# Weight loads on SP, a DMA pipe in the planner, and another order of layer 2's attention sessions

## The chip, the cores and the metric

The kernel runs on one core of one Trainium2 chip. The metric is the device time of one execution in microseconds (us), lower is better. Names of engines: PE multiplies matrices (TensorE), ACT computes exponentials and other functions (ScalarE), DVE works on vectors (VectorE), POOL is GpSimd, SP issues transfers (SyncE).

## The reference, cut to what matters

```python
def reference(A_x, A_wqkv, A_wo, B_x, B_w1, B_w2, B_w3, B_w4):
    # A(x): 16 heads of 28, softmax(q k^T / sqrt(28)) v, then @ wo        x: 1 x 2048 x 448
    # B(x): h = gelu(layernorm(x) @ w1); the four quarters of h's columns are shifted
    #       by -1, +1, -2, +2 rows; x1 = x + shifted @ w2
    #       x1 + gelu(layernorm(x1) @ w3) @ w4                            w3: 448 x 1792
    x = A_x
    x = x + A(layernorm(x))
    x = x + B(layernorm(x))
    x = x + A(layernorm(x))        # the same weights again
    x = x + B(layernorm(x))
    return x
```

So there are two layers, each an attention over 2048 rows and a mixing MLP. All data are bfloat16 in memory; `gelu` is the tanh form.

## The kernel before, in words

**Tiles.** The 2048 rows are 16 tiles of 128. Heads are padded from 28 to 32 rows, so four heads fill 128 partitions; the 16 heads are four groups g = 0 to 3. Queries are taken in chunks of up to 512 columns (`CHUNKS`: tiles 0-3, 4-7, 8-11, 12-13, 14-15), keys in chunks of their own (`KC`; in layer 2 tiles 0-2, 3-6, 7-10, 11-12, 13-15).

**Scores and exponentials.** A block is 128 keys (256 for the two half-width query chunks) of one head against one query chunk: 128 x 512 scores. The kernel has 2048 such blocks. PE writes the scores to PSUM (L1353) and an exponential turns them into bfloat16 weights (L1591). The blocks go in *units*: an even unit takes three PSUM banks (0-2), an odd unit two (3-4), and one ACT instruction handles a unit. A unit's scores wait until the exponential of the unit before last has read its banks, so PE is at most two units ahead. PE then multiplies the weights with the values (L802, `t_pv`).

**Blocks on DVE.** A few blocks get their exponential from DVE, in five instructions (`d_first`, `d_chain`: L1435, L1462, L1464, L1466, L1469). `D_RATE` says how many per query chunk; they use banks 6 and 7. `R_RATE` gives further ones, which borrow bank 2 of an even unit, so that this unit has two blocks for ACT and one for DVE.

**Sessions.** `ORDER` lists for each layer triples (query chunk, first key tile, end of key tiles). Each triple gives four sessions, one per head group; the kernel has 68, numbered from 0, and layer 2 begins at session 32. A session over part of the keys leaves partial sums: they are spilled to memory (`uscr<-ub`) and reloaded (`ub<-uscr`) when the next session of the same queries runs. The softmax uses an upper bound of the scores instead of their maximum. It is made from the largest key norms of all key chunks that the session touches or has touched (`t_bias`, L1295 to L1302). When a later session of the same queries needs the bound over more chunks, the queries are shifted by the difference first (`t_db`, `t_qp`, L1326, L1328, L1375). A key chunk therefore goes through projection on PE, eviction by DVE (L1152), squares on POOL (L1138), sums on PE and a maximum on DVE (L1165) before the first session with its bound can start.

**From layer 1 to layer 2.** When a tile leaves layer 1's MLP (`t_w4`: products with w4, residual sum L2035), its mean and variance are taken (L990, L991, and L996, L998 on POOL), it is normalized (L1005), transposed by a DMA issued by SP (L1015, or L1123 through memory) and projected to keys and values of layer 2 (`k_proj`, `v_proj`).

**MLP.** `t_mixA` and `t_mixB` make h and the w3 product. While attention runs, the GELU of a whole tile group is one long ACT instruction (L2019), with loads of function tables around it; h goes through tanh (L1839), whose table holds the exponential too. After the last exponential (the tail) the GELU works directly on PSUM (L1994).

**What sets the order.** Nothing is ordered by hand. When the kernel is built, a planner (`Sched.run`) runs all these routines as coroutines against a list of durations and readiness times, picks the next instruction for each engine by readiness and rank (`RANK`, `Q_LEAD`), and so fixes one instruction list per engine, with semaphore waits. On the chip each engine works through its list in order. Where the planner expects PE to idle, it inserts fillers (L2065), small matmuls whose result is unused. `LSEG` names the sessions whose start releases the clearing of the padded wo and the two groups of weight loads. Each transfer has an issue time and a time to landing in the planner, independent of other transfers.

Of the kernel before, what the change touches and what calls it, by code (L numbers as in the profile page):

```python
# [184 lines left out]
class Sched:  # L185
# [12 lines left out]
    def __init__(self, P):  # L198
# [17 lines left out]
        self.port = {"dve": (0.0, 0.0), "pool": (0.0, 0.0)}  # L216
        self.fill = None
# [167 lines left out]
    def run(self):  # L385
        P = self.P
        while True:
# [141 lines left out]
ORDER = {0: [(0, 0, 4), (1, 0, 4), (0, 4, 8), (0, 8, 16), (1, 4, 16), (2, 0, 16), (3, 0, 16), (4, 0, 16)], 1: [(0, 0, 7), (1, 0, 7), (0, 7, 11), (1, 7, 11), (0, 11, 16), (1, 11, 16), (2, 0, 16), (3, 0, 16), (4, 0, 16)]}  # L529
# [8 lines left out]
R_RATE = {(0, 0): 0, (0, 1): 0.03, (0, 2): 0.01, (0, 3): 0.02, (0, 4): 0, (1, 0): 0, (1, 1): 0, (1, 2): 0, (1, 3): 0.01, (1, 4): 0}  # L538
RLO = 5
RHI = 7  # L540
RPRIO = 0.5
# [4 lines left out]
DHI = 8  # L546
DPK = 2
RANK = {('q', 0, 1): 1.1, ('b', 0, 1): 1.254, ('b', 0, 0): 2.155, ('a', 0, 0): 1.411, ('k', 1, 0): 1.354, ('q', 0, 3): 1.199, ('k', 0, 1): 1.4, ('k', 1, 2): 1.381, ('k', 0, 2): 1.351, ('b', 0, 3): 2.679, ('q', 0, 2): 2.465, ('a', 0, 1): 1.751, ('k', 1, 1): 1.553, ('q', 1, 0): 1.781, ('k', 0, 3): 1.671, ('q', 1, 1): 2.16, ('a', 0, 2): 1.954, ('k', 1, 4): 1.95, ('a', 0, 4): 1.128, ('a', 0, 3): 1.842, ('b', 0, 4): 2.343, ('b', 0, 2): 2.033, ('a', 1, 0): 2.46, ('b', 1, 0): 1.514, ('a', 1, 3): 2.355, ('b', 1, 4): 1.667, ('a', 1, 2): 2.471, ('k', 1, 3): 2.435, ('a', 1, 1): 2.773, ('q', 1, 2): 2.611, ('b', 1, 2): 2.547, ('a', 1, 4): 2.738, ('b', 1, 3): 2.923, ('q', 1, 3): 2.432, ('b', 1, 1): 2.728, ('c', 0, 1): 1.22, ('w', 0, 1): 1.216, ('c', 0, 0): 1.023, ('w', 0, 0): 1.428, ('o', 0, 0): 1.775, ('v', 1, 0): 2.261, ('l', 1, 0): 2.465, ('v', 0, 1): 2.442, ('v', 1, 2): 1.73, ('l', 1, 2): 2.614, ('v', 0, 2): 1.5, ('c', 0, 3): 1.184, ('w', 0, 3): 1.412, ('o', 0, 1): 2.321, ('v', 1, 1): 1.973, ('l', 1, 1): 1.656, ('v', 0, 3): 2.178, ('o', 0, 2): 1.033, ('v', 1, 4): 2.482, ('l', 1, 4): 1.02, ('o', 0, 4): 1.711, ('o', 0, 3): 1.677, ('c', 0, 4): 2.197, ('w', 0, 4): 2.472, ('c', 0, 2): 2.133, ('w', 0, 2): 2.065, ('o', 1, 0): 1.617, ('c', 1, 0): 2.936, ('w', 1, 0): 1.115, ('o', 1, 3): 1.429, ('c', 1, 4): 2.839, ('w', 1, 4): 2.075, ('o', 1, 2): 2.017, ('v', 1, 3): 1.122, ('l', 1, 3): 2.584, ('o', 1, 1): 2.122, ('c', 1, 2): 2.188, ('w', 1, 2): 2.465, ('o', 1, 4): 2.837, ('c', 1, 3): 2.566, ('w', 1, 3): 2.092, ('c', 1, 1): 2.723, ('w', 1, 1): 2.8}
Q_LEAD = {(0, 1): 10, (0, 2): 5, (0, 3): 6, (1, 0): 4, (1, 1): 8, (1, 2): 5, (1, 3): 9}
D_RATE = {(0, 0): 0.11, (0, 1): 0.1, (0, 2): 0.07, (0, 3): 0, (0, 4): 0, (1, 0): 0.005, (1, 1): 0.105, (1, 2): 0.03, (1, 3): 0.02, (1, 4): 0}  # L550
PE_NORM = {(0, 0): False, (0, 1): False, (0, 2): False, (0, 3): False, (0, 4): False, (1, 0): False, (1, 1): False, (1, 2): False, (1, 3): True, (1, 4): True}
TANHW = {(0, 0): 0, (0, 3): 0, (0, 7): 0, (0, 11): 0, (0, 13): 0, (1, 0): 0, (1, 3): 0, (1, 7): 0, (1, 11): 0}
# [8 lines left out]
LSEG = (4, 7, 9)  # L561
POOLED = ('sq', 'otn', 'z2', 'xx')
GMERGE = {}
WARM = 0.5
# [9 lines left out]


def DRATE(L, ch, g):
    return D_RATE.get((L, ch), 0)

# [5 lines left out]
def build_kernel(nc, A_x, A_wqkv, A_wo, B_x, B_w1, B_w2, B_w3, B_w4, out, n_layers=2):  # L584
# [79 lines left out]
    with st:  # L664
# [103 lines left out]
        def op(eng, dur, fn, reads=(), writes=(), **kw):  # L768
            if eng == "pool" or (eng == "dve" and kw.pop("two", False)):
                kw["port"] = True  # L770
            return (eng, dur, fn, list(reads), list(writes), kw)
# [52 lines left out]
        def t_load():  # L824
# [24 lines left out]
            yield ("wait", ("segstart", LSEG[1]))  # L849
            for j in range(4):  # L850
                yield dma("pool", lambda e, j=j: e.dma_start(out=wo_pad[32 * j:32 * j + DH, :, :], in_=wo_v[j]), reads=[("woz",)], writes=[(("wo_pad",), j)], t=8.0, iss=0.7)
            yield dma("pool", lambda e: e.dma_start(out=w1[:, 0:3, :], in_=B_w1[0:384, :].rearrange("(c p) n -> p c n", p=128)), writes=[(("w1",), 0)], t=8.0, iss=0.7)
            yield dma("pool", lambda e: e.dma_start(out=w1[0:64, 3, :], in_=B_w1[384:448, :]), writes=[(("w1",), 1)], t=8.0, iss=0.7)
            yield dma("pool", lambda e: e.dma_start(out=w2[:, :, :], in_=B_w2.rearrange("(c p) n -> p c n", p=112)), writes=[("w2",)], t=8.0, iss=0.7)
# [158 lines left out]
        def tr_dma(slot, xt, i):  # L1013
            k = num(slot)
            return dma("sp", lambda e: e.dma_start_transpose(out=xv(xt)[:, :, 128 * i:128 * i + 128], in_=xn[:, k, :]),  # L1015
                       reads=[("xn", k)], writes=[(("xT", xt), i)], t=TR_T, iss=1.2, touch=[slot])
# [294 lines left out]
        def t_fct(L, p, pp):  # L1311
            i = PI[L, (pp, p)]
            for g in range(4):
                yield ("spawn", t_db(L, p, pp, g), 1)
# [850 lines left out]
```

## Time and profile before

| what | us |
|---|---|
| median of 3 runs (lowest, highest) | 1064.53 (1062.19, 1065.12) |
| the profiled execution | 1063.28 |
| its span in the profile | 1061.5 |
| ACT busy | 1007.3 (95%) |
| PE busy, fillers included | 990.9 (93%) |
| DVE busy | 680.6 (64%) |
| POOL busy | 306.0 (29%) |

Read busy times as averages: the kernel has a start, a long middle of attention with MLP work between, and a tail without exponentials. A row of a group gives line, engine, operation, output and inputs with shapes, count, then busy time, mean length of one in ns, and the idle time before these instructions with what ended it. The 40 digits of an engine are its busy tenths in 40 equal slices of the span.

### The profile page before, as it was taken

Reading aid. Unit: us, or ns where it says so; the run is one execution under the profiler, and the core shown is the slowest. Engines: PE = TensorE matmul, PEld = TensorE weight load, DVE = VectorE, ACT = ScalarE, POOL = GpSimd, SP = SyncE. Lnnn points to the kernel's source line nnn. Section 1 sums busy time; section 2 is a strip of 40 time slices with the busy share of each in tenths; the row PEclk is TensorE's granted clock in tenths of the full one; section 3 lists DMA queues with packets and bytes.
Section 4 is the critical chain, followed back from the end, with each engine's and each line's share of the span. In section 5 each row is a group of like instructions: output and inputs, shape, how many; then the busy total and the mean of one; then the engine's idle time right before and its main releaser. Section 6 shows DMA issues by size and latency. Waiting matters only on the chain.

```text
span 1061.5 us, 35381 instructions
## 1 busy us (share of the span) xinstructions
PE 990.9 (93%) x15980; PEld 410.0 (39%) x15983; DVE 680.6 (64%) x1365; ACT 1007.3 (95%) x913; POOL 306.0 (29%) x507
## 2 busy tenths in 40 slices
PE   8898998999999999999999989998989999899998
PEld 4332342333424334434432333343333343444465
DVE  7674797788568757776457445747778536565442
ACT  7998999999999999999999999999999999999952
POOL 2342112434232304453234111103554300432111
PEclk9999999999999999999999999999999999999999
DMA  4547232402121103231132114334412110121000
GB/s 117 130 117 202 76 72 68 62 22 37 21 75 41 33 12 86 63 52 23 33 78 74 44 52 129 104 76 116 74 23 32 32 39 25 34 66 25 12 21 24
DMA packets 96443, 64.22 MB, mean 61 GB/s; under 512 B 68580, under 2 KB 85172, under 8 KB 96292
## 3 DMA queue, kind: packets, MB, share of 16 engines
q1 hardware_dynamic: 92916, 53.88, 21.1%
q0 software_dynamic: 3376, 8.09, 2.8%
q8 instruction: 125, 2.05, 0.8%
q14 instruction: 26, 0.21, 0.1%
HBM read 28.03 MB, written 16.76 MB: 42 GB/s over the span
## 4 chain that ended last, share of the span: by engine, by line
ACT 72%; PE 20%; DMA 3%; DVE 3%; issue 1%; SPq 1%; POOL 0%; DVEq 0%
ACT PT L1591 66%; PE ps L811 11%; PE ps L1353 4%; PE ps L802 3%; ACT h2T L2019 2%; DMA xT<-xnd 2%; ACT fb L1839 1%; PE ps L2065 1%; ACT L2019 1%; DMA xT<-xn 1%; ACT L1591 1%; DVE fb L1462 0%; DMA rT<-ub 0%; DMA PT<-in_A_wqkv_dram 0%; SPq L1015 0%
## 5 line engine op out<-in xcount | busy, mean ns | idle before, releaser
L1591 ACT ACTIVATE PT<-ps 128x1024 bf16<-128x1024 f32 (+1 forms) x802 | 910.4, 1340 | 15.5 <-PE ps L1353 14.8
L1353 PE MATMUL ps<-qT,kT 32*128 32x512 bf16 (+1 forms) x2560 | 315.2, 341 | 36.8 <-ACT PT L1591 28.4
L802 PE MATMUL ps<-PT,vaug 128*32 128x512 bf16 (+1 forms) x2491 | 250.9, 342 | 0.8 <-ACT PT L1591 0.5
L1353 PEld LDWEIGHTS ps<-qT,kT 32*128 32x128 bf16 x2560 | 80.6, 91 | 317.6 <-ACT PT L1591 285.1
L811 PE MATMUL ps<-xT,w 128*32 128x512 bf16 (+4 forms) x2368 | 160.9, 345 | 5.8 <-DMA xT<-xn 4.0
L2065 PE MATMUL ps<-ident 128*32 128x256 bf16 x3212 | 145.9, 279 | 4.2 <-DVE hT L1820 2.4
L802 PEld LDWEIGHTS ps<-PT,vaug 128*32 128x32 bf16 x2491 | 74.2, 95 | 93.4 <-issue 76.8
L2065 PEld LDWEIGHTS ps<-ident 128*32 128x32 bf16 x3212 | 90.8, 98 | 31.9 <-issue 13.1
L811 PE MATMUL ps<-w,h2T 128*32 128x448 bf16 x1288 | 90.5, 358 | 5.7 <-ACT h2T L2019 5.7
L1696 POOL TENSOR_TENSOR otn<-ub,fb 128x512 bf16<-128x512 f32 (+1 forms) x35 | 39.9, 1139 | 187.7 <-DMA fb<-rscr 187.7
L1998 DVE CAST h2T<-ps 128x384 bf16<-128x384 f32 (+1 forms) x84 | 52.2, 622 | 50.8 <-PE ps L811 50.0
L811 PEld LDWEIGHTS ps<-xT,w 128*32 128x32 bf16 (+1 forms) x2368 | 64.6, 96 | 50.1 <-issue 27.2
L1138 POOL TENSOR_TENSOR sq<-kT 128x512 bf16<-128x512 bf16 (+2 forms) x32 | 31.2, 981 | 94.7 <-DVE kT L1152 80.4
L1837 POOL TENSOR_TENSOR fb<-hT 112x512 f32<-112x512 bf16 (+1 forms) x36 | 37.8, 1054 | 61.7 <-DVE hT L1820 53.7
L811 PEld LDWEIGHTS ps<-w,h2T 128*32 128x32 bf16 x1288 | 36.0, 97 | 34.9 <-issue 15.2
L811 PE MATMUL ps<-xT,wk_pad 128*32 128x512 bf16 (+2 forms) x576 | 44.6, 366 | 3.1 <-DMA xT<-xnd 3.0
L1923 POOL TENSOR_TENSOR x_res<-x_res,x1b 128x448 f32<-128x448 f32 x32 | 38.2, 1199 | 32.1 <-DVE xn L1010 32.1
L1435 DVE TENSOR_SCALAR yd<-ps 128x512 int32<-128x512 f32 x43 | 29.5, 687 | 25.6 <-PE ps L1353 25.2
L1138 POOL TENSOR_TENSOR sq<-qT 128x512 bf16<-128x512 bf16 x28 | 30.6, 1100 | 43.2 <-DVE qT L1187 36.2
L811 PE MATMUL ps<-wo_pad,otn 128*32 128x448 bf16 x512 | 39.5, 356 | 2.9 <-DVE x_res L1750 1.6
L811 PE MATMUL ps<-w,hT 112*32 112x448 bf16 x512 | 41.2, 355 | 0.5 <-DVE x1b L1908 0.5
L811 PE MATMUL ps<-xT,wq_pad 128*32 128x512 bf16 x448 | 39.3, 388 | 1.4 <-DMA xT<-xnd 0.9
(183 smaller groups left out, 1190.3 us busy)
## 6 DMA issues: line engine op xcount, KB each, us to landing
uscr<-ub SPq DMA_DIRECT2D x28, 256.0 KB, 2.0
ub<-uscr SPq DMA_DIRECT2D x28, 256.0 KB, 4.0
fb<-rscr SPq DMA_DIRECT2D x24, 256.0 KB
xnd<-xn SPq DMA_DIRECT2D x28, 128.0 KB, 2.1
x_res<-in_A_x_dram POOLq DMA_DIRECT2D x16, 224.0 KB, 2.7
xd<-x_res SPq DMA_DIRECT2D x16, 224.0 KB, 2.9
x_res<-xd SPq DMA_DIRECT2D x16, 224.0 KB, 3.6
out_dram<-obf SPq DMA_DIRECT2D x16, 112.0 KB, 1.7
```

Of the source, the lines that this page charges most:

```text
L802: return lambda e: e.matmul(out=out, lhsT=lhsT, rhs=rhs, start=start, stop=stop, **kw)
L811: r.append(e.matmul(out=out[c:c + w, :], lhsT=lhsT[:, c:c + w], rhs=rhs, start=start, stop=stop, tile_position=(0, c)))
L1138: return both("sq", 0.15 + NW * 0.0018, 0.07 + NW * 0.00104, lambda e: e.tensor_tensor(out=sq[:, si, 0:NW], in0=src, in1=src, op=ALU.mult) ...
L1353: yield op("pe", (0.005 + NW * 0.00042) / nc_, lambda e, i=i, kc=kc, j=j, g=g, a=a, NW=NW, bank=bank: e.matmul(out=ps[:, bank, i * NW:(i + ...
L1435: yield op("dve", c_ps(512), lambda e: e.tensor_scalar(out=y, in0=ps[:, bi(bank), :], scalar1=SCALE * L2E * FS, scalar2=-126.0 * FS, op0=A ...
L1591: yield op("act", 0.06 + n * w * 0.000833, lambda e, bk=bk, s0=s0, n=n, w=w: e.activation(out=PT[:, s0:s0 + n, 0:w], in_=ps[:, bk[0]:bk[0] ...
L1696: yield both("otn", 0.2 + NW * 0.0021, 0.07 + NW * 0.00104, lambda e: e.tensor_tensor(out=otn[:, g, 0:NW], in0=u, in1=rb[:, 0:NW], op=ALU. ...
L1837: yield both("z2", 0.2 + NW * 0.00165, 0.07 + NW * 0.00104, lambda e: e.tensor_tensor(out=f, in0=z, in1=z, op=ALU.mult), hk, [fk])
L1923: yield both("xx", 1.2, 0.54, lambda e: e.tensor_tensor(out=X, in0=X, in1=X1, op=ALU.add), [xk, ("x1b", s)], [xk], deps=[nop_])
L1998: ev = op("dve", c_ps(m * NW), lambda e, hr=hr, pv=pv: e.tensor_copy(out=hr, in_=pv), reads=[("ps", bi(b))], writes=hk, touch=[b])
L2019: yield op("act", c_act(len(fr_) * NW), lambda e, v=v: e.activation(out=v, in_=v, func=ACT.Gelu_apprx_tanh), reads=allk, writes=allk, tab= ...
L2065: return [e.matmul(out=ps[32 * c:32 * c + 32, bi(b), 0:256].rearrange("p (a n) -> p a n", n=128), lhsT=ident[:, 32 * c:32 * c + 32], rhs=i ...
```

## The change

- The four loads of wo, the three of w1 and w2, and the three of w3 and w4 are issued by SP instead of POOL; they start at sessions 6 and 10 instead of 7 and 9 (`LSEG`).
- The planner gets one DMA pipe: a transfer with a service time `svc` lands no earlier than the pipe has served it behind all others, and a transpose (`hold`) keeps its queue until the pipe is free.
- Layer 2's sessions (0,7,11), (1,7,11), (0,11,16) become (1,7,11), (0,7,16): 32 sessions in layer 2 instead of 36, 64 in all.
- In layer 2 the bounds and their differences are made for the four head groups together (`t_bias4`, `t_fct`) instead of one by one.
- `D_RATE` and `R_RATE` are given for each pair of sessions instead of each query chunk. Ranks, leads and some planner constants have other values; `DHI` lets a DVE block be chosen one step further ahead.
- `POOLED` keeps only the squares of keys and queries on POOL; three other operations may go to DVE where the planner finds that earlier.
- `TANHW[0, 11]`: the tile group 11, 12 of layer 1 takes the tanh form for its second GELU.
- `ONCE` is empty, so the branches that it opens are not used.

```diff
+        self.pipe = 0.0
...
             if dma:
-                self.cur[eng] = start + kw.get("iss", 0.35)
+                svc = kw.get("svc", 0.0)
+                self.cur[eng] = start + kw.get("iss", 0.4)
                 t_end = start + kw.get("dma_time", 3.0)
+                if svc:
+                    if kw.get("hold"):
+                        self.cur[eng] = max(self.cur[eng], self.pipe)
+                    self.pipe = max(self.pipe, start + 1.2) + svc
+                    t_end = max(t_end, self.pipe + 1.2)
...
-ORDER = {... 1: [(0, 0, 7), (1, 0, 7), (0, 7, 11), (1, 7, 11), (0, 11, 16), (1, 11, 16), (2, 0, 16), (3, 0, 16), (4, 0, 16)]}
+ORDER = {... 1: [(0, 0, 7), (1, 0, 7), (1, 7, 11), (0, 7, 16), (1, 11, 16), (2, 0, 16), (3, 0, 16), (4, 0, 16)]}
...
-DPRIO = 1.5
+DPRIO = 2
...
-R_RATE = {(0, 0): 0, (0, 1): 0.03, ...}
+R_RATE = {(0,): 0, (1,): 0.03, ..., (31,): 0}
...
-RPRIO = 0.5
+RPRIO = 1
...
-DHI = 8
+DHI = 9
...
-D_RATE = {(0, 0): 0.11, (0, 1): 0.1, ...}
+D_RATE = {(0,): 0.1, (1,): 0.125, ..., (31,): 0.12}
...
-TANHW = {... (0, 11): 0, ...}
+TANHW = {... (0, 11): 1, ...}
...
-LSEG = (4, 7, 9)
-POOLED = ('sq', 'otn', 'z2', 'xx')
+LSEG = (4, 6, 10)
+POOLED = ('sq',)
...
             yield ("wait", ("segstart", LSEG[1]))
+            yield ("wait", ("woz",))
             for j in range(4):
-                yield dma("pool", lambda e, j=j: e.dma_start(out=wo_pad[...], in_=wo_v[j]), ..., t=8.0, iss=0.7)
+                yield dma("sp", lambda e, j=j: e.dma_start(out=wo_pad[...], in_=wo_v[j]), ..., t=5.0, svc=0.35, iss=0.55)
...
             yield ("wait", ("segstart", LSEG[2]))
-            yield dma("pool", ... w3[:, 0:3, :] ..., t=16.0, iss=0.7)
+            yield dma("sp", ... w3[:, 0:3, :] ..., t=5.0, svc=4.9, iss=0.55)
...
+        def t_bias4(L, p):
+            yield ("wait", ("rtn",))
+            for g in range(4):
+                for c in range(p):
+                    yield ("wait", ("k", L, g, c))
...
+            if p > 1:
+                yield op("dve", 0.14, ... reduce_max(out=k2[:, L, p, :], in_=kmaxc[:, L, :, 0:p], axis=AX.X), ...)
...
+            yield op("dve", 0.13, ... tensor_tensor(out=sc[:, 5, :], in0=src, in1=RTN, op=ALU.mult), ...)
+            yield op("dve", 0.13, ... tensor_scalar(out=bcb[:, L, p, :], in0=sc[:, 5, :], scalar1=WSH, ...), ...)
+            yield op("dve", 0.13, ... tensor_scalar(out=bc29[:, L, p, :], in0=bcb[:, L, p, :], scalar1=M29, ...), ...)
+            for g in range(4):
+                yield ("sig", ("bc", L, p, g))
...
-                    rate = rates.get((L, ch), 0)
+                    rate = rates.get((si // 2,), 0)
```

More of the change, by code (lines that the diff above doesn't have):

```diff
@@ L560 @@
 SMALL = [11, 12]
[L561 to L562 removed]
+LSEG = (4, 6, 10)
+POOLED = ('sq',)
 GMERGE = {}
+ONCE = {}
 WARM = 0.5
@@ L1123, in load_xT @@
             yield dma("sp", lambda e: e.dma_start_transpose(out=xv(xt)[:, :, 0:128 * n], in_=xnd[128 * t0:128 * (t0 + n), :]),
-                      reads=[("xnd", t) for t in range(t0, t0 + n)], writes=[(("xT", xt), i) for i in range(4)], t=TRL_T, iss=2.2)
+                      reads=[("xnd", t) for t in range(t0, t0 + n)], writes=[(("xT", xt), i) for i in range(4)], t=TRL_T, svc=1.02 * n, hold=True, iss=2.2)
         def proj(xt, g, wpad, wnm, NW=512):
@@ L1790, in t_mixA @@
             t0 = tiles[0]
+            once = ONCE.get((L, tiles[0]), 0) and not direct
             for t in tiles:
```

98 lines of the change are left out of this document (68 added, 30 removed).

## The prediction

> **What bounds the kernel now.** I read the page first, then the groups with their shapes kept apart, the waits and the windows of ScalarE.
>
> ```profile
> span 1061.5 us, 35381 instructions
> PE 990.9 (93%) x15980; PEld 410.0 (39%) x15983; DVE 680.6 (64%) x1365; ACT 1007.3 (95%) x913; POOL 306.0 (29%) x507
> DVE  7674797788568757776457445747778536565442
> ACT  7998999999999999999999999999999999999952
> ACT 72%; PE 20%; DMA 3%; DVE 3%; issue 1%; SPq 1%; POOL 0%; DVEq 0%
> ```
>
> Two engines are above 90%, but they are not alike. ACT carries 72% of the chain that ended last and is full in every slice but the first, the fourth and the last two. PE's 93% holds fillers: L2065, multiplications of the identity with itself that nobody reads. So a microsecond of ACT work in the middle is a microsecond of the kernel, as long as ACT is fed.
>
> ```profile
> ACT PT L1591 <- PE ps L1353: 14.8, 18, 2.9
> ACT h2T L1994 <- PE ps L811: 11.8, 3, 9.0
> ACT PT L1994 <- PE ps L811: 9.8, 14, 7.8
> ```
>
> The exponentials (L1591) wait 14.8 us in all for scores (L1353). The other two rows belong to the tail, after the last exponential, where PE leads.
>
> ```profile
> 636.00:689.00 53.00, 49.85 (x755) 19.46 (x745) 32.33 (x75) 52.99 (x50) 6.08 (x10) 1.00 0.39 114
> 1007.00:1061.50 54.50, 49.92 (x1158) 31.83 (x1154) 19.13 (x39) 21.77 (x30) 9.60 (x21) 1.00 0.07 22
> ```
>
> Columns: stretch, its length, then busy time of PE, PEld, DVE, ACT and POOL. The first row is where layer 2's reordered sessions lie: ACT is busy 52.99 of 53.00 us, so the present order feeds it without a gap. DVE has 20 us to spare there.
>
> **The change part by part.** The planner runs when the kernel is built, so the order of every instruction of the changed kernel can be counted. Against the kernel before:
>
> *Fewer exponentials on ACT.* DVE takes 89 of the 2048 score blocks (128x512) instead of 61: 46 instead of 40 in layer 1, 43 instead of 21 in layer 2. ACT issues 360 exponentials of 1536 elements instead of 383, 439 of 1024 instead of 419, and one of 512.
>
> ```profile
> L1591 ACT ACTIVATE PT<-ps 128x1536 bf16<-128x1536 f32 x383 | 599.2, 1564 | 10.2 <-PE ps L1353 9.6
> L1591 ACT ACTIVATE PT<-ps 128x1024 bf16<-128x1024 f32 x419 | 470.5, 1135 | 5.2 <-PE ps L1353 5.2
> L2019 ACT ACT_TABLE_LOAD x8 | 10.3, 1283 | 0.1
> L1591 ACT ACTIVATE PT<-ps 128x1024 bf16<-128x1024 f32 (+1 forms) x802 | 910.4, 1340 | 15.5 <-PE ps L1353 14.8
> L1839 ACT ACTIVATE fb<-fb 112x512 f32<-112x512 f32 x24 | 16.1, 692 | 0.0
> L2019 ACT ACTIVATE vaug<-vaug 128x3584 bf16<-128x3584 bf16 x2 | 6.4, 3192 | 0.0
> ```
>
> Neighbouring exponentials overlap: the two forms sum to 1069.7 us, but all 802 together keep ACT busy for 910.4, so each costs 0.2 us less than its mean: 1.36, 0.93 and, one 0.43 step lower, 0.50 us. That gives -23 x 1.36 + 20 x 0.93 + 0.50 = -12.2 us.
>
> *Tile pair 11, 12 of layer 1 takes tanh instead of GELU (TANHW).* One GELU of 3584 elements goes (-3.2), two table loads go (-2.6), seven tanh of 512 elements come (7 x 0.49 = +3.4, same overlap). With two tiny exponents more: -2.3 us. ACT work before the tail falls by 14.5 us; I take 14, since part of the overlap is lost next to other functions.
>
> *What DVE pays.*
>
> ```profile
> L1435 DVE TENSOR_SCALAR yd<-ps 128x512 int32<-128x512 f32 x43 | 29.5, 687 | 25.6 <-PE ps L1353 25.2
> L1462 DVE SCALAR_TENSOR_TENSOR fb<-yd 128x512 f32<-128x512 uint16 x38 | 28.3, 746 | 2.2 <-POOL otn L1696 1.8
> L1464 DVE SCALAR_TENSOR_TENSOR fb<-fb,yd 128x512 f32<-128x512 f32 x38 | 27.0, 712 | 0.4
> L1466 DVE TENSOR_SCALAR PD<-fb 128x512 bf16<-128x512 f32 x45 | 20.3, 453 | 0.6
> L1469 DVE SCALAR_TENSOR_TENSOR PD<-yd,PD 128x512 int16<-128x512 int16 x40 | 28.5, 713 | 0.7
> ```
>
> A block costs DVE 3.3 us, 28 of them 93 us. Residual additions and squares that POOL did before (L1923, L1837: 12 and 9) and two more steps for each of seven tanh chains are 35 instructions of the 0.7 us of these rows, 25 us. DVE goes from 64% to about 75%: off the path on average, and the spare time of layer 2 covers it. Without that cover: 40 units instead of 18 now lend bank 2 to such a block, and the unit after next waits until DVE has read it (0.69 us). With DVE late by half an instruction on 22 more units the cost would be 7 us, with DVE on time 0; before, 18 such units belong to a total wait of 14.8 us with startup in it, so I take +0.5.
>
> *Layer 2's sessions.* (0,7,11) and (0,11,16) become one, (0,7,16), behind (1,7,11): 32 sessions, four spills and four reloads fewer, all hidden. But session 44 now is the first of (0,7,16), and its queries are shifted by the bound over all five key chunks. The last chunk holds tiles 13 to 15, the end of layer 1. Before, session 44 was (1,7,11), needing three chunks; the last one was due at session 48. The combined bound (t_bias4) also waits for all four head groups. In the planned order nothing but two small exponents stands on ACT between the last exponential of session 43 (unit 513) and the first of session 44, while PE has all of chunk 4's key projections and the V projections there. So ACT will stop; how long is the main question.
>
> ```profile
> 651.37 0.62 DVE L2035 TENSOR_TENSOR x_res<-x_res,ps 128x448 f32<-128x448 f32 x1 [2.77 <-PE ps L811]
> 654.66 0.51 DVE L1005 TENSOR_SCALAR xn<-x_res,mv,rstd 128x448 bf16<-128x448 f32 x1
> 663.28 1.14 DVE L1152 TENSOR_SCALAR kT<-ps,cols 128x384 bf16<-128x384 f32 x2
> 674.73 0.55 DVE L1165 TENSOR_REDUCE kmaxc<-ps 128x1 f32<-128x384 f32 x1
> 676.50 0.61 DVE L1232 CAST vaug<-ps 128x448 bf16<-128x448 f32 x1
> 677.75 0.21 DVE L1328 TENSOR_SCALAR db<-dbc,cols 128x1 f32<-128x1 f32 x1
> 677.99 0.35 DVE L1375 TENSOR_SCALAR qT<-qT,db 128x512 bf16<-128x512 bf16 x1
> 663.97 1.61 POOL L1138 TENSOR_TENSOR sq<-kT 128x384 bf16<-128x384 bf16 x2 [10.14 <-DVE kT L1152]
> 660.33 1.04 PE L811 MATMUL ps<-xT,wk_pad 128*32 128x384 bf16 x16
> xT<-xn SPq DMA_TRANSPOSE x56, 2.5
> ```
>
> These are the steps of tile 15 before: its residual sum (651.37), its norm (done 655.17), the transpose (2.5 us to landing), the keys, their squares on POOL, the maxima (last done 675.28), the shift of the queries. From the sum to the last shifted constant 26.6 us pass, unhurried. Pressed together: 3.8 to the norm, 2.5 landing, 1.0 first projection, 0.6 eviction, four squares at 0.8 (3.2), sums and maximum 0.9, bias, two V casts and the query shift 3.1, scores 0.4: 15.5 us, and 2 more if squares wait for their two buffers. In the new order the sum stands at unit 507, so ACT still has 508 to 513 to do: three of each size, 6.9 us. That leaves a stop of 8.6 to 10.6 us. The lower end is PE's: 45 groups of four matmuls (25 for keys, 20 for values) at 0.22 us (0.26 in the row above, where scores stand between) are 10 us between the scores of 513 and 514, less two units that are scored ahead, 2.3: 7.6. The upper end is the unhurried chain, 26.6 - 6.9 = 19.7. I take +10, near the compressed chain, as those instructions stand directly behind each other now.
>
> *Weight loads.* Ten loads move from POOL (29% busy, off the path) to SP, the first seven to session 6 instead of 7, the last three (w3 in two parts, w4) to session 10 instead of 9. What counts is the neighbour.
>
> ```profile
> 35.69 2.00 SPq L1123 DMA_TRANSPOSE xT<-xnd  x1
> 86.05 7.14 SPq L1123 DMA_TRANSPOSE xT<-xnd  x1
> w<-in_B_w_dram POOLq DMA_DIRECT2D x1, 1568.0 KB, 12.7
> ub<-uscr SPq DMA_DIRECT2D x28, 256.0 KB, 4.0
> 96.47 1.45 ACT L1591 ACTIVATE PT<-ps 128x1536 bf16<-128x1536 f32 x1 [2.93 <-PE ps L1353]
> 100.11 3.71 ACT L1591 ACTIVATE PT<-ps 128x1536 bf16<-128x1536 f32 x3 [0.68 <-PE ps L1353]
> ```
>
> Before, w3 and w4 were issued with the last key transpose of layer 1; that transpose held SP 7.14 us instead of 2.00, and ACT lost 3.6 us just behind it. Now the transpose is issued eight units (9 us) ahead of w3, so that stop should go. Late next is session 10's reload of partial sums: it stands on SP right behind w4 (12.7 us to land), 11 units (12.5 us) ahead of the DVE instruction that needs it; DVE, and behind it PE's next session, may wait 1 to 4 us, of which two scored units hide 2.3. Between -3.6 and +1.7 I take -2.5, the earlier transpose being the surer half. The Trainium skill (DMA: Bandwidth & Descriptors, "Issuing engines are not separate DMA queues") says that DMAs of all issuing engines interleave on the same sixteen engines and that another issuer saves only issue time; the stretched transpose agrees. By that rule the move to SP itself is worth nothing, and if the loads met a transpose again the sum would be 2.5 us higher.
>
> *The tail.* At the last exponential three of fourteen w3 parts of tiles 7 to 10 are still to come: 36 matmuls of 512 columns and 12 of 256 more.
>
> ```profile
> 1006.90 0.73 PE L811 MATMUL ps<-xT,w 128*32 128x512 bf16 x16
> 1016.39 9.45 PE ps L811 x196
> 1041.59 17.09 PE ps L811 x392
> ```
>
> The chain through the tail is PE's; 36 x 0.046 + 12 x 0.03 = 2.0 us. It could be 0 if they fill the wait for the GELU, or 4 if three ACT pieces delay that too: +2.0.
>
> *The rest.* The new ranks, leads and rates move other work among the 800 units; ACT's full slices hide that unless a score comes late. At the start the first query transpose is issued at unit 15 instead of 13; between 0 and the 2 us of two units I take 0, since its queries are due at unit 25 as before.
>
> **Sum:** 1063.28 - 14.0 + 0.5 + 10.0 - 2.5 + 2.0 = 1059.3 us. That profiled execution is 1.25 us under the median of the three runs (1064.53).
>
> **The rivals.**
> 1. *The handoff runs at its old, unhurried pace.* For it: those instructions wait on four engines in turn, each in its own order, and a late DVE pushes all. Against: DVE and PE have nothing else to do then. Stop 19.7 instead of 10: 1069.0, slower. From a stop of 17 us on the kernel is slower by over 0.3%.
> 2. *The handoff is hidden.* If tile 15 is ready earlier (the faster layer 1 frees DVE and PE), the stop falls to 4 us: 1053.3. Against: the order of PE puts 10 us of projections there whatever comes in early.
> 3. *DVE becomes the feeder.* 22 more borrowed banks and fuller DVE cost 7 us instead of 0.5: 1065.8, no change. For it: the first half of DVE's slices already stands at 7 and 8. Against: most new blocks lie in layer 2, where they are 3 to 5.
> 4. *Session 10's reload takes the place of the transpose's stop* (+1.7 instead of -2.5): 1063.5.
>
> **How the numbers follow.** 0.3% (3.2 us) is about what a measurement of this kernel can tell from no change: faster is below 1061.3, slower above 1067.7. The forecast has 0.45, its own range being 1056 to 1062 (stop of 7 to 13), two thirds of it faster; rival 2 has 0.20, all faster; rival 1 has 0.17 and rival 3 0.13, half of which ends slower with some of each added; rival 4 has 0.05. Faster: 0.30 + 0.20 = 0.50; slower: 0.17 + 0.07 = 0.24, and the rest, 0.26, is the same. The range of 1051 to 1069 reaches over rivals 2 to 4 and up to rival 1.
>
> **What would show it.** ACT busy near 993 us, with 799 to 801 exponentials; one gap of about 10 us in ACT between 640 and 670 us, ended by PE's scores, with the key squares on POOL inside it; no gap of 3 us near 95; a transpose near 2 to 5 us there; about 54 us from the last exponential to the end; DVE near 75%. The prediction is wrong if that gap is below 6 or above 17 us, or if ACT's waits outside it and the tail grow beyond 20 us.

## The result, and the profile after

| what | before | changed |
|---|---|---|
| median, us | 1064.22 | 1055.15 |
| lowest to highest, us | 1060.73 to 1065.23 | 1052.06 to 1058.9 |
| ratio (95% interval) | | 0.9921 (0.9895 to 0.9947) |
| the profiled execution, us | 1063.28 | 1058.90 |

The kernel is faster by 9.1 us (0.8%). The two profiled executions are only 4.4 us apart: that of the changed kernel is its slowest, with a dip of the granted clock near its end. A second profiled execution of the same kernel (1055.18 us, "control" below) is near the median. First the page of the changed kernel: span, busy times, and ACT's and the clock's digits in 40 slices.

```profile
span 1057.1 us, 35265 instructions
PE 987.8 (93%) x15871; PEld 408.6 (39%) x15871; DVE 775.9 (73%) x1498; ACT 993.3 (94%) x919; POOL 294.2 (28%) x480
ACT  7999999999999999999999995999999999999943
PEclk9999999999999999999999999998999999999899
```

ACT has 14.0 us less to do than before (1007.3), DVE is at 73% instead of 64%. One slice of ACT, the 25th, shows a 5: a new stop. ACT's waits in the changed kernel (what waited, for what; us in all, times, longest):

```profile
ACT h2T L2046 <- PE ps L817: 18.5, 6, 8.2
ACT fct L1339 <- DVE dbc L1353: 12.3, 1, 12.3
ACT PT L1632 <- PE ps L1394: 10.8, 15, 1.8
```

The second row is the stop, a single wait of 12.3 us. The exponentials (L1632) wait less for scores than before (10.8 against 14.8 us); most of that is the early stop near 95 us, which held 4.1 of the 14.8. To see where the rest went, the windows by stretch: stretch, length, busy time of PE, PEld, DVE, ACT and POOL, then granted clock, DMA share, GB/s. Before:

```profile
75.00:125.00 50.00, 44.53 (x597) 15.01 (x589) 29.06 (x80) 45.80 (x44) 10.79 (x13) 0.97 0.55 161
125.00:350.00 225.00, 208.21 (x3097) 79.79 (x3091) 177.17 (x308) 218.62 (x197) 69.82 (x108) 0.98 0.23 48
600.00:700.00 100.00, 93.30 (x1467) 37.60 (x1455) 54.96 (x118) 99.83 (x87) 10.12 (x18) 1.00 0.31 91
700.00:940.00 240.00, 223.96 (x3572) 90.94 (x3569) 151.92 (x271) 238.81 (x212) 77.75 (x128) 0.99 0.23 50
```

The changed kernel, with one more row near its end:

```profile
75.00:125.00 50.00, 47.64 (x685) 17.40 (x677) 35.91 (x87) 49.94 (x48) 10.79 (x12) 1.00 0.56 158
125.00:350.00 225.00, 207.52 (x3110) 80.66 (x3102) 186.85 (x325) 221.35 (x202) 74.70 (x112) 0.99 0.23 50
600.00:700.00 100.00, 90.89 (x1485) 37.85 (x1477) 74.09 (x144) 86.76 (x79) 11.54 (x20) 1.00 0.28 78
700.00:940.00 240.00, 221.15 (x3439) 86.82 (x3439) 183.20 (x329) 236.71 (x211) 74.82 (x125) 0.98 0.19 45
940.00:1003.00 63.00, 60.81 (x994) 27.83 (x994) 34.00 (x72) 61.00 (x58) 12.01 (x25) 0.95 0.12 26
```

The control in its last stretch of exponentials:

```profile
940.00:1003.00 63.00, 60.72 (x1038) 29.40 (x1035) 34.26 (x74) 62.92 (x62) 10.91 (x24) 1.00 0.14 28
```

ACT's idle time is length less busy time. Together with the stretches that are not quoted:

| ACT idle, us | before | changed | control |
|---|---|---|---|
| 0 to 75 | 9.1 | 7.8 | 8.2 |
| 75 to 125 | 4.2 | 0.1 | 0.1 |
| 125 to 350 | 6.4 | 3.7 | 2.5 |
| 350 to 600 | 0.4 | 0.3 | 0.3 |
| 600 to 700 | 0.2 | 13.2 | 13.2 |
| 700 to 940 | 1.2 | 3.3 | 3.5 |
| 940 to the end | 32.8 | 35.5 | 33.4 |
| ACT busy | 1007.3 | 993.3 | 992.3 |
| span | 1061.5 | 1057.1 | 1053.5 |

So 14 to 15 us of work went, about 9 us of small stops in the first 350 us went too (before to control), and one stop of 13 us came. From the last exponential to the end it is 53.7 us instead of 52.7.

The stop is the handoff from layer 1 to layer 2. In the timeline of the changed kernel (start, length, engine, line, operation, tiles, count; in brackets idle before and its releaser), DVE's part first, beginning with tile 15's residual sum:

```profile
635.48 0.62 DVE L2087 TENSOR_TENSOR x_res<-x_res,ps 128x448 f32<-128x448 f32 x1 [3.55 <-PE ps L817]
638.28 0.50 DVE L1013 TENSOR_SCALAR xn<-x_res,mv,rstd 128x448 bf16<-128x448 f32 x1
645.37 0.61 DVE L1160 TENSOR_SCALAR kT<-ps,cols 128x384 bf16<-128x384 f32 x1
652.16 1.18 DVE L1173 TENSOR_REDUCE kmaxc<-ps 128x1 f32<-128x384 f32 x2
655.18 0.23 DVE L1353 TENSOR_TENSOR dbc<-bcb 128x4 f32<-128x4 bf16 x2
```

Then PE and ACT:

```profile
649.50 0.50 PE L2117 MATMUL ps<-ident 128*32 128x256 bf16 x12
654.44 1.16 PE L2117 MATMUL ps<-ident 128*32 128x256 bf16 x24
656.05 0.60 PE L1394 MATMUL ps<-qT,kT 32*128 32x512 bf16 x5 [0.45 <-DVE qT L1416]
635.16 7.96 ACT L1632 ACTIVATE PT<-ps 128x1024 bf16<-128x1024 f32 x7
655.38 0.30 ACT L1339 ACTIVATE fct<-dbc 128x4 f32<-128x4 f32 x2 [12.25 <-DVE dbc L1353]
656.49 3.71 ACT L1632 ACTIVATE PT<-ps 128x1536 bf16<-128x1536 f32 x3 [0.81 <-PE ps L1394]
```

From the sum at 635.48 to the scores at 656.05 are 20.6 us; ACT's work ended at 643.12, 7.6 us after the sum. The stop is 13.1 us (12.25 and 0.81), without the two small exponents in it. PE is not full: it runs 36 fillers (L2117) in the stop.

Not all of the 20.6 us is spent on tile 15. Its transpose is issued at 638.84 and lands 2.6 us later, but PE's first projection of those keys stands at 643.40, behind work on the chunk before. From there the chain that ended last (start, length, engine, tile, line, count) goes to and fro between two engines. A part of it:

```profile
645.51 0.86 PE ps L817 x16
646.39 0.63 DVE kT L1160
647.07 0.86 PE ps L817 x16
647.96 0.63 DVE kT L1160
648.63 0.97 PE ps L817 x16
649.62 0.64 DVE vaug L1240
650.39 1.21 PE ps L817 x20
651.62 0.63 DVE vaug L1240
```

From 643.54 to the last of these casts (ended 655.14) this chain holds 7.2 us of PE, 3.8 us of DVE and 0.6 us between them. No square on POOL and no transfer is on it. The releasers of such a chain are inferred, so the experiments below test it.

### The profile page after: what moved, and what is told of

It is laid out like the page before. It is cut to its first block, busy times and chain, and to the rows that moved or that the text cites. A ratio compares the mean times of both kernels' runs of the same rounds, so it can differ in the third digit from the quotient of the medians.

```text
span 1057.1 us, 35265 instructions
## 1 busy us (share of the span) xinstructions
PE 987.8 (93%) x15871; PEld 408.6 (39%) x15871; DVE 775.9 (73%) x1498; ACT 993.3 (94%) x919; POOL 294.2 (28%) x480
## 4 chain that ended last, share of the span: by engine, by line
ACT 76%; PE 18%; DVE 3%; DMA 2%; issue 0%; SPq 0%; DVEq 0%
ACT PT L1632 69%; PE ps L817 11%; PE ps L1394 4%; ACT h2T L2071 3%; PE ps L808 3%; ACT fb L1891 2%; DMA xT<-xnd 1%; ACT L1632 1%; ACT L2071 1%; DVE fb L1503 1%; DMA PT<-in_A_wqkv_dram 0%; DVE yd L1476 0%; PE ps L2117 0%; DVE vaug L1240 0%; ACT sq L1143 0%
## 5 line engine op out<-in xcount | busy, mean ns | idle before, releaser
L1632 ACT ACTIVATE PT<-ps 128x1024 bf16<-128x1024 f32 (+1 forms) x800 | 900.5, 1330 | 13.5 <-PE ps L1394 10.8
L817 PE MATMUL ps<-xT,w 128*32 128x512 bf16 (+4 forms) x2592 | 178.0, 346 | 2.5 <-DVE hT L1863 1.7
L2117 PE MATMUL ps<-ident 128*32 128x256 bf16 x3100 | 146.2, 280 | 3.0 <-POOL ident L898 1.5
L2117 PEld LDWEIGHTS ps<-ident 128*32 128x32 bf16 x3100 | 88.8, 98 | 32.7 <-issue 12.6
L817 PEld LDWEIGHTS ps<-xT,w 128*32 128x32 bf16 (+1 forms) x2592 | 70.8, 95 | 51.5 <-issue 23.7
L1476 DVE TENSOR_SCALAR yd<-ps 128x512 int32<-128x512 f32 x64 | 44.0, 687 | 26.1 <-PE ps L1394 25.5
L1889 POOL TENSOR_TENSOR fb<-hT 112x512 f32<-112x512 bf16 (+1 forms) x27 | 33.5, 1240 | 54.4 <-DVE hT L1863 42.3
L1510 DVE SCALAR_TENSOR_TENSOR PD<-yd,PD 128x512 int16<-128x512 int16 x61 | 43.2, 711 | 1.2
L1503 DVE SCALAR_TENSOR_TENSOR fb<-yd 128x512 f32<-128x512 uint16 x59 | 43.2, 738 | 0.4
L1505 DVE SCALAR_TENSOR_TENSOR fb<-fb,yd 128x512 f32<-128x512 f32 x59 | 40.9, 697 | 0.7
```

The costliest lines, as they stand in the source:

```text
L817: r.append(e.matmul(out=out[c:c + w, :], lhsT=lhsT[:, c:c + w], rhs=rhs, start=start, stop=stop, tile_position=(0, c)))
L1476: yield op("dve", c_ps(512), lambda e: e.tensor_scalar(out=y, in0=ps[:, bi(bank), :], scalar1=SCALE * L2E * FS, scalar2=-126.0 * FS, op0=A ...
L1503: yield op(D_[0][0], D_[0][1], lambda e: e.scalar_tensor_tensor(out=q, in0=lo, scalar=E2 / E3 * FS, in1=lo, op0=ALU.add, op1=ALU.mult), re ...
L1505: yield op(D_[1][0], D_[1][1], lambda e: e.scalar_tensor_tensor(out=q, in0=q, scalar=E1 / E3 * FS * FS, in1=lo, op0=ALU.add, op1=ALU.mult) ...
L1510: yield op(D_[3][0], D_[3][1], lambda e: e.scalar_tensor_tensor(out=pdt.bitcast(I16), in0=hi, scalar=128.0, in1=pdt.bitcast(I16), op0=ALU. ...
L1632: yield op("act", 0.06 + n * w * 0.000833, lambda e, bk=bk, s0=s0, n=n, w=w: e.activation(out=PT[:, s0:s0 + n, 0:w], in_=ps[:, bk[0]:bk[0] ...
```

## The experiments

### The handoff: session order, bounds and the chain through the last tile

**The old order of sessions, all else as changed (e1).** The rates of a session pair move with its queries.

```diff
-ORDER[1]: ..., (1, 7, 11), (0, 7, 16), (1, 11, 16), ...
+ORDER[1]: ..., (0, 7, 11), (1, 7, 11), (0, 11, 16), (1, 11, 16), ...
```

> The changed kernel with layer 2's sessions in the order of the kernel before: (0,7,11), (1,7,11), (0,11,16), four sessions more again; the rates of each session pair move with their queries, everything else stays. Theory: the changed kernel's ACT stop of 12.3 us before session 44 comes from asking for the bound over all five key chunks four sessions too early. In the old order the last chunks are due at session 48, about 25 units (29 us) later, so the stop goes and no other takes its place: ACT waits for scores stay near 12 us in all, the shift factor's wait (L1339 in the changed kernel, 12.3 us) falls below 2 us, and the time falls by 9 to 13 us against the changed kernel's 1055.2, to 1042 to 1046. Rival: tile 15 itself, or PE's 45 groups of key and value projections, set the time, and the stop only moves to session 48, in the plan the scores of session 48 stand directly behind those projections: a stop of 8 to 12 us there, time 1052 to 1056. Second rival: what the four sessions more cost (spills, reloads, their shifts) is not hidden: 1049 or more without any stop above 3 us.

Measured: 1086.66 us, ratio to the kernel before 1.0216 (1.0191 to 1.0242), 3% slower than the changed kernel. None of the three cases gave that. ACT's waits and its digits:

```profile
ACT fb L1891 <- DVE fb L1890: 33.4, 1, 33.4
ACT fct L1339 <- DVE dbc L1353: 8.0, 1, 8.0
ACT  7999999999999999999999996999999999998023
```

The stop shrank to 8.0 us and moved to session 48, and the last exponential ended at 992.6 instead of 1003.4 us. But the planner, which plans every instruction anew after any edit, left a whole tanh chain behind the last exponential: the tail grew from 54 to 94 us (the zero among ACT's last digits, and the wait of 33.4 us). One edit of a constant moved two things here, and the time alone would have told the wrong story.

**The old order with five other ranks (e5).** They concern only layer 2's key chunks 3 and 4.

```diff
-('k',1,3): 2.403, ('k',1,4): 1.498, ('v',1,3): 2.638, ('v',1,4): 1.832, ('l',1,4): 2.454
+('k',1,3): 1.441, ('k',1,4): 2.589, ('v',1,3): 1.665, ('v',1,4): 2.632, ('l',1,4): 1.201
```

> The old session order again, with five ranks of the planner changed (keys and values of layer 2's chunks 3 and 4, norm of the tiles of chunk 4), which move nothing ahead of layer 2's last key chunks. In the first old-order run the last exponential ended 10.8 us earlier than in the changed kernel, but the planner had left 40 us more work in the tail (94 instead of 54 us). Theory: that tail is an accident of the planner's choices and not a price of the order; with the tail back at 53 to 56 us and the stop at session 48 between 0 and 6 us the time is 1043 to 1048. Rival: the order needs the longer tail, because the four sessions more leave less room for the MLP work before the end: the tail stays above 65 us and the time above 1056.

Measured: 1049.33 us, ratio 0.9881 (0.9865 to 0.9897); the tail is 52.8 us. The long tail was the planner's choice, not the price of the order. The handoff, with the shift factor no longer waited for:

```profile
668.93 0.28 ACT L1339 ACTIVATE fct<-dbc 128x4 f32<-128x4 f32 x1
670.51 4.62 ACT L1632 ACTIVATE PT<-ps 128x1536 bf16<-128x1536 f32 x4 [1.30 <-PE ps L1394]
```

A stop of 1.3 us is left. The time is 1.3 us above the theory's range; where that went was not separated, though in the profiled execution ACT lost 4.4 us in a stretch from 790 to 830 us with a granted clock of 0.91.

**The old order, bounds per head group, and ranks (e6).**

```diff
-                if L == 1:
-                    SC.spawn(t_bias4(L, e_), 1)
-                    continue
```

and in `t_fct` the four differences `t_db` for both layers. Ranks: 2.302, 1.003, 1.385, 1.669, 1.479 in the order above.

> The old session order, bounds made per head group as in the kernel before, and the same five ranks with other values. Theory: no stop is left at the handoff (the first group's keys of the last two chunks are projected at least seven units ahead), the tail is 53 to 56 us: 1039 to 1044, faster than both kernels by about 2%. Rival: what the 12 us stop cost comes back as many small waits for scores, since DVE and PE lose the rest that the stop gave them: 1048 or more, with ACT's waits for scores above 20 us.

Measured: **1041.78 us**, ratio 0.9807 (0.9794 to 0.982): faster than both kernels: by 1.9% than the kernel before and, by the two ratios, by 1.1% than the changed one. Its page and its waits:

```profile
PE 978.2 (94%) x15684; PEld 402.0 (39%) x15687; DVE 766.0 (74%) x1500; ACT 995.4 (96%) x918; POOL 304.0 (29%) x488
ACT PT L1631 <- PE ps L1393: 7.7, 11, 1.8
```

No wait for scores is longer than 1.8 us. DVE does almost the same work as in the changed kernel (766.0 against 775.9 us), so its load alone does not make the stop; the small waits did not come back. The tail is 50.5 us, shorter than expected.

**The new order with the same bounds and the same five ranks (e12).** Against the kernel just above, only `ORDER` differs, with the rates that follow the queries.

> The changed kernel's session order with bounds per head group and the same five ranks as the fastest kernel so far (old order, 1041.8 us): the two differ in the session order alone. Theory: the order costs the stop of 12 to 13 us and little else: 1054 to 1060, ACT stopped for 9 to 14 us before session 44. Rival: the ranks make the difference, and with them the new order runs without a stop above 6 us: 1043 to 1050.

Measured: 1059.2 us, ratio 0.9956 (0.9942 to 0.9971), 17.4 us above its twin; the theory's time held. The stop:

```profile
656.65 5.54 ACT L1631 ACTIVATE PT<-ps 128x1024 bf16<-128x1024 f32 x5 [14.29 <-PE ps L1393]
```

14.3 us, at the first scores of session 44. In the profiles the last exponential ends 11.9 us later than in the twin and the tail is 3.2 us longer. This pair shows the price of the new order with equal bounds and ranks: the order of sessions was the part of the change that cost time. The planner still orders the rest anew in each of the two, so 17.4 us is the price in this pair and not a constant.

**The new order with bounds per group, ranks as changed (e2).** The edit to `t_bias4` and `t_fct` alone.

> The changed kernel with layer 2's bounds and differences made for each of the four head groups by itself, as in the kernel before; the order stays. Theory: the stop before session 44 is a chain through the last tile and through PE's projections; the first group's keys need only 4 + 5 of the 45 groups of matmuls ahead of the scores, so waiting for one group instead of four saves three quarters of the squares (3 of the 4 at 0.8 us) and part of PE's work: the stop falls from 12.3 to 6 to 9 us and the time to about 1049 to 1052. Rival: the four groups' reductions, which come 0.5 us apart, are not what is waited for (the chain up to the first key projection is), and the stop stays at 11 to 13 us: 1054 to 1056.

Measured: 1058.84 us, ratio 0.9958 (0.9942 to 0.9974); no gain, and a time above both cases. The stop is 13.1 us, at the upper end of the rival's 11 to 13, but for another reason:

```profile
642.32 0.62 DVE L2086 TENSOR_TENSOR x_res<-x_res,ps 128x448 f32<-128x448 f32 x1 [2.78 <-PE ps L817]
655.77 0.38 PE L1393 MATMUL ps<-qT,kT 32*128 32x512 bf16 x1
```

From tile 15's sum to the scores it is now 13.5 us instead of 20.6: the chain is 7 us shorter. But in this plan the sum itself comes 7 us later, so ACT stops just as long. Since the whole plan is new, how much of the 7 us comes from waiting for one group instead of four is not shown. Here the chain that ended last does pass through tile 15's sum.

**Small squares in the same planned order (e10).** Only the size of one kind of instruction changes, not the plan.

```diff
-    e.tensor_tensor(out=sq[:, si, 0:NW], in0=src, in1=src, op=ALU.mult)
+    e.tensor_tensor(out=sq[:, si, 0:W], in0=src[:, 0:W], in1=src[:, 0:W], op=ALU.mult)   # W = 32 for layer 2, chunk 4
```

> The changed kernel with the same planned order, but the squares of layer 2's last key chunk on POOL take 32 of 384 columns (0.2 to 0.3 us instead of 0.83), so the bound comes from old squares in the rest: part of the computation is left out. Theory: the stop before session 44 is the chain of tile 15, as in the prediction's sum, in which four squares stand behind each other: 12.3 us falls to 9.5 to 10.8. Rival: PE's list sets it (projections, sums and V projections in one order with banks that DVE empties), and squares are waited for little: 11.5 to 12.8 us.

Measured: 1055.84 us, ratio 0.9931 (0.9911 to 0.9951). The last square and the stop:

```profile
649.57 0.24 POOL L1147 TENSOR_TENSOR sq<-kT 128x32 bf16<-128x32 bf16 x1 [0.82 <-PE ps L817]
654.12 0.30 ACT L1340 ACTIVATE fct<-dbc 128x4 f32<-128x4 f32 x2 [12.25 <-DVE dbc L1354]
```

A square takes 0.24 instead of 0.83 us, and the stop is 12.25 us as before, to the digit. POOL just waits the difference longer for PE (0.82 instead of 0.23 us). The squares are not on the path.

**Small value projections in the same planned order (e11).**

```diff
+            W = 64 if L == 1 and c >= 3 else D
-  mm4(ps[:, bi(b), 0:D], ..., wv[:, fc, :], ...)
+  mm4(ps[:, bi(b), 0:W], ..., wv[:, fc, 0:W], ...)
```

> The changed kernel with the same planned order, but layer 2's value projections of the last two key chunks take 64 of 448 columns: 20 groups of four matmuls, about 0.2 us each, become a fourth of that, so part of the values is left out. Theory (tile 15's chain sets the stop): value projections fill PE between the sums of the key groups, the stop stays within 1 us of 12.3. Rival (PE's list sets it): 2 to 4 us less, 8.5 to 10.3.

Measured: 1054.73 us, ratio 0.9916 (0.9897 to 0.9934).

```profile
652.27 0.30 ACT L1340 ACTIVATE fct<-dbc 128x4 f32<-128x4 f32 x2 [10.55 <-DVE dbc L1354]
```

The stop falls by 1.7 us, between the two cases: PE's value projections are on the path, with 1.7 of 12.3 us. The end did not move (span 1053.7 against the control's 1053.5). Session 44 starts 1.7 us earlier than in the control, session 56 at the same time; from 657 to 940 us ACT is idle for 4.6 instead of 3.5 us, with a granted clock of 0.96 instead of 0.98 up to 700 us. The rest of the chain was not taken apart by a run. By the chain shown above it is PE's key projections and sums in turn with DVE's evictions and casts, in the order of their lists; no experiment changed that order alone.

### The weight loads

**The kernel before with the ten loads on SP and the new sessions (e4).** After such an edit the planner also reorders some DVE and PE instructions, here between about 75 and 110 us, against what the expectation says; ACT keeps its order.

```diff
-LSEG = (4, 7, 9)
+LSEG = (4, 6, 10)
-            yield dma("pool", ... wo_pad, w1, w2, w3, w4 ..., iss=0.7)
+            yield dma("sp", ... wo_pad, w1, w2, w3, w4 ..., iss=0.55)
```

> The kernel before with only the ten weight loads moved to SP and started at sessions 6 and 10 instead of 7 and 9; order of all other instructions as before. Theory: w3 and w4 no longer meet the last key transpose of layer 1, the stop of 3.6 us at 94 to 101 us goes, nothing replaces it: 1060 to 1061 against 1064.2, and the transpose near 86 us holds SP 2 to 3 us instead of 7.1. Rival: session 10's reload of partial sums, now behind w4 on SP, stops DVE and then ACT by 1 to 4 us just after: 1062 to 1066. Second rival: the load already in flight with the first seven (from session 6) hits another transpose: no change, 1064.

**The same with the loads still on POOL (e8).** Only `LSEG`. Apart from the ten loads the order of instructions on ACT, DVE, POOL and SP is the same in both, so these two differ in the issuer of the loads alone.

> The kernel before with its weight loads still on POOL, but started at sessions 6 and 10 instead of 7 and 9: the other half of the run that moved them to SP. There, ACT lost 2.9 us between 75 and 125 us instead of 5.2 (stop behind the transpose gone, one of 2.3 us at 108 to 111 in its place). Theory: the start of the loads did that, not the issuer: the transpose near 86 us holds SP 2 to 3 us, ACT loses 2 to 4 us in that stretch, and the time is that of the SP run within 1.5 us (1061 to 1063). Rival: the loads on POOL do not stand ahead of session 10's reload on SP, so the second stop is missing too: ACT loses less than 1 us there, 1059 to 1061. Second rival: the issuer made the gain, and the 3 to 4 us stop is back at another transpose or reload: 1063 or more.

Measured: on SP 1062.31 us, ratio 0.9991 (0.9977 to 1.0005); on POOL 1064.4 us, ratio 1.0023 (1.0007 to 1.0039). The loads on SP are 0.3% better than on POOL with the same `LSEG`; the theory that the start does it and not the issuer fell, and the second rival held. Against the kernel before, the loads on SP are no clear gain by themselves (the interval holds 1). The windows from 75 to 125 us show ACT idle for 4.2 us before, 2.3 us with the loads on SP and 4.1 us with them on POOL; the expectation of the run on POOL has 5.2 and 2.9 for the first two. On SP (e4), the transpose, the spill ahead of the loads, w4, and then two waits behind session 10's reload:

```profile
85.01 1.96 SPq L1125 DMA_TRANSPOSE xT<-xnd  x1
91.48 0.32 SPq L1680 DMA_DIRECT2D uscr<-ub  x1
92.91 0.59 SPq L859 DMA_DIRECT2D w<-in_B_w_dram  x1
105.73 0.75 DVE L1674 SCALAR_TENSOR_TENSOR ub<-ub,fct,ps 128x512 f32<-128x512 f32 x1 [2.13 <-DMA ub<-uscr]
110.94 2.37 ACT L1593 ACTIVATE PT<-ps 128x1536 bf16<-128x1536 f32 x2 [1.57 <-PE ps L1355]
```

On POOL (e8):

```profile
78.50 0.82 POOL L856 DMA_DIRECT2D w<-in_B_w_dram  x1
85.31 5.59 SPq L1123 DMA_TRANSPOSE xT<-xnd  x1
95.80 2.39 ACT L1591 ACTIVATE PT<-ps 128x1536 bf16<-128x1536 f32 x2 [2.75 <-PE ps L1353]
```

`LSEG` names a session in the plan, and the chip does not wait for it: POOL has nothing in its list that holds it back, so w3 left at 78.50 us though the plan puts it at session 10; the first scores of session 8 are at 79.6 and those of session 10 at 98.9. It ran into the transpose, which held SP for 5.59 us, and the old stop stayed. On SP the same load stands behind the spill of a session, which cannot leave before that session's sums exist; it left after the transpose. On SP, half of what that stretch gained went to the reload, as the first rival of that run said: DVE waits 2.13 us for it and ACT 1.57 us for the scores behind. In the changed kernel the stop is gone without a replacement (0.1 us idle from 75 to 125).

### The work taken from ACT

**The rates before for blocks on DVE (e3).**

```diff
-D_RATE, R_RATE: per session pair (89 blocks)
+D_RATE, R_RATE: the values before, per query chunk (64 blocks)
```

> The changed kernel with the rates of the kernel before for blocks on DVE (by query chunk): 64 blocks instead of 89 go to DVE, ACT issues 385 exponentials of three blocks and 414 of two. Theory: in the middle a microsecond of ACT work is a microsecond of the kernel, so the 25 blocks come back on ACT as 25 x 0.43 = +11 us: about 1066, of 1064 to 1068. Rival: the further blocks on DVE cost as much in waits for DVE as they save on ACT (the waits of exponentials for scores were 10.8 us in the changed kernel and would fall by some microseconds): 1055 to 1060.

Measured: 1069.0 us, ratio 1.0058 (1.0038 to 1.0077), 14 us above the changed kernel.

```profile
PE 995.5 (93%) x16307; PEld 419.3 (39%) x16307; DVE 703.6 (66%) x1376; ACT 1006.1 (94%) x918; POOL 285.1 (27%) x480
ACT fct L1339 <- DVE dbc L1353: 4.8, 1, 4.8
```

ACT has 12.8 us more to do and the time rises by about as much, 1 us above the theory's range; the rival falls. ACT's idle time is the same in sum (62.1 us, 61.2 in the control), but it lies elsewhere. The stop is 4.8 instead of 12.3 us, with 6.6 us more of ACT work, exponentials, ahead of it (637.3 against 630.7 us): ACT work in front of a stop that other engines time is partly free. In its place ACT waits 5.85 us for scores near 499 us and idles 38.9 instead of 33.4 us after 940. So blocks on DVE pay, but that they pay in full is not shown: the new plan's other stops are in the 14 us.

**The tile group 11, 12 back on the long GELU (e7).**

```diff
-TANHW = {... (0, 11): 1, ...}
+TANHW = {... (0, 11): 0, ...}
```

> The changed kernel with the tile group 11, 12 of layer 1 on the long GELU again. The prediction put the tanh form at -2.3 us of ACT work. Theory: ACT is the bound in that stretch, so 1.5 to 3 us come back: 1056.5 to 1058.5 against 1055.2, ACT with two table loads more and seven tanh less. Rival: the seven tanh chains cost PE and DVE what ACT gains (two more DVE steps each) and nothing is seen: within 1 us of the changed kernel, or even faster.

Measured: 1052.93 us, ratio 0.9915 (0.9903 to 0.9928): no difference from the changed kernel (0.9921 and 0.9922), so the rival's time held. The wait that answers to the stop:

```profile
ACT fct L1339 <- DVE dbc L1353: 8.2, 1, 8.2
```

The work that the tanh form saved lies just ahead of the handoff, and the stop without it is 4 us shorter: that, and not the rival's load on PE and DVE, is what the trace shows. This term of the change was worth nothing.

### The changed kernel again

**Unchanged, as control (e9).**

> The changed kernel as it is, once more, as the control of this group. Its profiled execution on record (1058.9 us) was the slowest of its six, with a granted clock of 0.95 from 940 to 1005 us, where another run of this group of kernels shows 1.00 and 3 us less between the start of the last query chunk and the last exponential. Theory: that was this execution alone: median 1053 to 1056, and in a new profile 58 to 59.5 us from the start of session 60 to the last exponential instead of 61.7, with the stop before session 44 again at 12 to 13.5 us. Rival: the kernel does this in most executions: 61 us or more again.

Measured: 1054.86 us, ratio 0.9922 (0.9902 to 0.9943). From the start of session 60 to the last exponential 59.2 us, the stop 12.25 us again. The dip of the clock to 0.95 belonged to the first profiled execution, the stop to the kernel.

## Why the prediction was right, and where it was not

The direction was right and 1055.15 us lies in the range; the forecast of 1059.3 was 4.1 us too high, and the gain that it forecast, 4.0 us on the profiled execution, is less than half of the 9.1 us measured. It agrees with the first profiled execution (1058.9), but only by luck, the dip of the clock; against the control the sum misses by as much as against the median. Point by point:

- *ACT work, -14.* Right: 1007.3 to 993.3 us (992.3 in the control), and the run with the old rates, with 12.8 us more work on ACT, takes 14 us longer, though its stops lie elsewhere. The part of it from the tanh group, -2.3, was right as ACT work and wrong as time: it was counted as a gain while it stands directly ahead of a stop which the same sum introduced two paragraphs later.
- *DVE's load, +0.5.* Right within what can be seen: outside the early stop (4.1 us) and the new one (0.8 us) the waits for scores went from 10.7 to 10.0 us (7.2 in the control). Rival 3 falls.
- *The handoff, +10.* Right in place, kind and sign, 3 us too small: 13.1 us. The step that failed is "Pressed together ... 15.5 us": to the scores the chain took 20.6. That sum went from tile 15's transpose straight into the projections, while the transposed tile lay ready for 2 us before PE came to it. It put four squares of 0.8 us in series, and shrinking them changes nothing. And it took DVE and PE as free for the chain, while PE's list puts value projections between the key groups' sums (1.7 us by the run that shrinks them) and DVE's casts stand between the maxima. ACT's remaining work was sized well (7.6 against 6.9 us). The lower end, PE's 10 us of projections in one piece, did not set the stop either: PE ran 36 fillers in it, and its groups came in turn with DVE, 7.2 and 3.8 us on the chain. Rival 1 asked for a stop of 19.7 us and rival 2 for 4: both fall, and rival 2's 1053.3 us is near the result for another reason.
- *The early stop, -2.5.* The gain was -4.1 us in that stretch. The surer half (transpose ahead of w3) was right, with 2.08 us for the transpose; the replacement by session 10's reload, which was to cost part of it, appears only when the loads are moved in the kernel before (there the net is -1.9: 2.3 instead of 4.2 us idle), not in the changed kernel. Rival 4 falls for this kernel. The statement that "the move to SP itself is worth nothing" does not hold between the two runs that differ in the issuer alone (0.3%). The Trainium skill (DMA: Bandwidth & Descriptors, "Issuing engines are not separate DMA queues") says that transfers interleave whichever engine started them, and the trace agrees: beside a load from POOL a transpose from SP took 5.59 us. It also says that another issuer saves only the time to issue, and here the measurement decides otherwise: the order in the issuer's list moved w3 from 78.50 to about 92 us, and that moved the time.
- *The tail, +2.* Measured +1.0 (52.7 to 53.7 us).
- *The rest, 0.* Of the terms that came out lower than forecast this one missed by most. Between 125 and 350 us ACT idles 2.5 us in the control instead of 6.4, of which the prediction had nothing; 0.9 us more went at the start, and 2.3 came between 700 and 940. With the order before, two other runs (e4, e8) idle 4.7 and 4.8 us from 125 to 350 us at a clock of 0.99, so perhaps half of the 3.9 us goes with the changed plan and the rest with the execution; that split is an estimate. Which of its edits does it was not tested.

Taken together against the control: work -1.0, stop +3.1, early stop -1.6, tail -1.0, DVE -0.5, the rest -2.5, which makes -3.5 of the -4.1 us. The single errors add up to 9.7 us without their signs: that the sum came within 4.1 us is in part luck, since the longer stop hid gains elsewhere.

## What to carry to other kernels

When an order of work is changed, ask for each step what its inputs were due for before: a session that needs the bound over all keys four sessions earlier turned a covered chain into a stop of 13 us, and putting the old order back (with bounds per head group and ranks that suit it) gave 1041.8 us, more than twice the gain of the whole change. Work saved on the bounding engine directly ahead of a stop is no gain, so the two terms must not be added. And where a planner orders everything anew, look at the whole profile of an experiment before its time is believed: the same edit gave 1086.7 us with one set of ranks and 1049.3 with another.

## What the runs showed of the hardware that was not expected

- The queue that issues a transfer decides when it goes, by what stands ahead of it: with the loads on POOL the start in the plan could be moved by a session without moving the load on the chip (79.68 us before, 78.50 in e8, both ahead of session 8's first scores), and a key transpose beside it held SP for 7.14 and 5.59 us; behind a spill on SP it left at about 92 us, and the transpose took 1.96 and 2.08 us.
- A granted clock of 0.95 over 63 us, with PE feeding ACT closely, went with 1.9 us less work of ACT in that stretch than at 1.00 in another execution of the same kernel (61.00 against 62.92 us busy). One profiled execution can differ by this from the median, more than several terms of a sum.
- Squares on POOL that took 0.24 instead of 0.83 us moved nothing at all, to a hundredth of a us: a chain over four engines can have a member that is always early, however serial its rows look.
